# Pair loads as one 128-partition transfer, and four early pairs loaded ahead of a weight, in an attention + channel-mix kernel

## The chip, the cores and the metric

The kernel runs on one core of one Trainium2 chip. The metric is the device time of one execution in microseconds (us), lower is better. Five engines work side by side, each through its own fixed list of instructions: PE (TensorE), DVE (VectorE), ACT (ScalarE), POOL (GpSimd) and SP (SyncE, which here only issues DMAs). A DMA can be issued from SP's or from ACT's instruction list ("SPq", "ACTq" in the rows).

## The reference

Inputs are q, k, v of 8 batches x 8 heads x 576 positions x 64, s (8 x 8 x 576), two mixing vectors and three float64 weights, w_k (512 x 1024), w_v (1024 x 512) and w_r (512 x 512).

```python
# attention, per batch and head
cum    = cumsum(maximum(s, 0))
bias   = minimum(-(cum[:, None] - cum[None, :]), 0)
scores = where(causal, -1e9, q @ k.T / sqrt(64) + bias)
attn   = softmax(scores)            # rows, with 1e-9 in the divisor
x      = concat_heads(attn @ v)     # (8, 576, 512)
# channel mix
xk = mu_k * x + (1 - mu_k) * shift(x);  xr = mu_r * x + (1 - mu_r) * shift(x)
out = sigmoid(xr @ w_r) * (maximum(xk @ w_k, 0) ** 2 @ w_v)
```

## The kernel before, in words

**Pairs and visits.** Heads are treated two at a time; a pair is two heads of one batch. `visits` (L1356) lists the work on attention: first the four pairs of batch 0 in two parts each, part A (query positions 0 to 319, visits 0 to 3) and then part Z (320 to 575, visits 4 to 7), then 28 whole pairs of batches 1 to 7. The 8 visits of batch 0 are "plain": q and k go to the scores matmul as float32 (L817), with the row of prefix sums of s as a 65th partition of k. The 28 others are "split" pairs: every operand is taken apart in a high and a low part, and two matmuls (L828) make the scores.

**Loads of a pair.** `load_plain` (L668) fills a tile "KH" and a tile "G", two buffers each, with k and q of a plain visit in partitions 0 to 63 (L681). For visit 0 each head is a transfer of its own, head 0 from ACT's queue and head 1 from SP's. Partition 64 of k is the prefix-sum row. Visit 0 makes its own from s (L675, scans at L700); visit 1 copies it from the scan over all heads (L530, DMA at L709); later visits read it back from the DRAM copy `whole_d` (written at L536, read at L716). `load_turned` (L723) fills a tile "raw" (two buffers, one for q and one for k) of a split pair: the same 64 rows go to partitions 0 to 63 and again to 64 to 127, in two transfers of 288 KB (L729). `split_qk` (L737) makes from them KH and G (ACT, L769 and L782) and the low parts KL and G (POOL, L773 and L796). KL and a second copy of q, G2, lie in four fixed tiles, two KL and two G2, whose upper 64 partitions are cleared and set once by `constant_rows` (six memsets on POOL, L507 and L510).

**Weights.** `load_weight` (L568) loads a block of 512 KB of float64 words (L578) and makes float32 high and low parts of it: one ACT instruction (L603), four on DVE (L608, L615, L619, L626), one on ACT (L632) and one on POOL (L634). There are 8 blocks of w_k, 4 of w_r and 8 of w_v.

**Attention and channel mix.** For each visit and head: scores on PE, a bias, mask and row minimum on DVE (L845), exponents on ACT (L863), normalization on POOL (L899, L877) with a reciprocal on DVE (L904), transposes on PE (L921, L935), values on PE (L1068 plain, L1082 split), result to DRAM (L1437). `channel_mix` (L1152) runs over 18 chunks of 256 positions: mixing on ACT and DVE (L1173, L1184), then matmuls with w_k (L1236), w_r (L1278) and w_v (L1303). Where PE would have nothing to do early on, filler matmuls on an identity (L425) are put in its list.

**Order.** Every instruction is a task of a planner (`Plan`). `forward` (L145) makes a list schedule from estimated durations and due times, `backward` (L262) gives new due times from it, and `run` (L309) takes the best of 40 rounds and emits the instructions in that order. So each engine, and SP's list of DMAs too, has one fixed order, found for the whole kernel at once. A set of dependencies for each task keeps the order legal; at L1476 the w_v loads are made dependent on the first load of x for chunk 0.

Of the kernel before, what the change touches and what calls it, by code (L numbers as in the profile page):

```python
# [54 lines left out]
class Plan:  # L55
# [14 lines left out]
    def __init__(self):  # L70
        self.tasks, self.slots, self.due = [], {}, 0.0
        self.columns, self.idle, self.busy_from = {}, None, None
        self.ports = {}
# [71 lines left out]
    def forward(self, due):  # L145
# [6 lines left out]
        start = [0.0] * n  # L152
        for i, (_, _, _, deps, _, _) in enumerate(self.tasks):
            missing[i] = len(deps)
            for d in deps:
                users[d].append(i)
        engines = list(dict.fromkeys(t[0] for t in self.tasks))
# [22 lines left out]
        while len(order) < n:  # L180
# [71 lines left out]
            order.append(i)  # L252
            for u in users[i]:
# [8 lines left out]
    def backward(self, start):  # L262
# [4 lines left out]
        for t in self.tasks:  # L267
            for d in t[3]:
# [8 lines left out]
        for _ in range(n):  # L277
# [17 lines left out]
            for d in deps:  # L295
                k, _, _, _, _, land = self.tasks[d]
                gap = self.SELF[k] if k == e and e != "SP" else self.AFTER[k] + self.BEFORE[e]
                if k == "SP" or k == "PE":
# [26 lines left out]
def forgetting_attention_then_channel_mix(  # L325
# [15 lines left out]
    nc = tc.nc  # L341

    B, H, D, S = q.shape
    DM, DF = moe_w_k.shape
    P = 128
    NP = H // 2
# [126 lines left out]
    late, LATE = [], ("v",)  # L473
# [11 lines left out]
    KLs = [fixed(const.tile([P, 2, S], F32R, name=f"KL{i}")) for i in range(2)]  # L485
    G2s = [fixed(const.tile([P, 2, S], F32R, name=f"G2{i}")) for i in range(2)]
    turns = [0]
# [80 lines left out]
    def load_weight(name, c, o, w, due, x):  # L568
# [17 lines left out]
        if name in LATE:  # L586
            late.append(i)
        plan.due = due
# [79 lines left out]
    def load_plain(n, src, b, hp, a, e, tag):  # L668

        x = sbuf([P, 2, e - a], tag, 2)  # L670
# [7 lines left out]
        for js in ((0, 1), (1, 2)) if n == 0 else ((0, 2),):  # L678
            first = n == 0 and js[0] == 0
            (dma if not first else aside)(  # L680
                lambda js=js, queue=nc.scalar if first else nc.sync: queue.dma_start(  # L681
                    x.get()[0:64, js[0] : js[1]],
                    src[b, 2 * hp + js[0] : 2 * hp + js[1], :, a:e].rearrange("h d t -> d h t"),
                ),
                [], [(x, (j, 0)) for j in range(*js)], 580 * (js[1] - js[0]) * (e - a) / S,
            )
        if tag == "G":
            if n < 2:
# [34 lines left out]
    def load_turned(src, b, hp, a, e, tag, apart):  # L723

        x = sbuf([P, 2, e - a], "raw", 2)
        for r in range(2):
            for js in ((0, 1), (1, 2)) if apart else ((0, 2),):
                dma(
                    lambda r=r, js=js: nc.sync.dma_start(  # L729
                        x.get()[64 * r : 64 * r + 64, js[0] : js[1]],  # L730
                        src[b, 2 * hp + js[0] : 2 * hp + js[1], :, a:e].rearrange("h d t -> d h t"),
                    ),
                    [], [(x, (j, r)) for j in range(*js)], 580 * (js[1] - js[0]) * (e - a) / S,
# [783 lines left out]
```

## Time and profile before

| | us |
|---|---|
| median of 3 runs | 862.51 (860.14 to 863.93) |
| the profiled execution's own time | 861.32 |
| its span (first to last instruction) | 859.5 |
| PE busy in the span | 844.3 |
| ACT / DVE / POOL busy | 668.0 / 654.6 / 425.8 |

In the rows, a time is in us from the start of the span. "Busy" of PE counts modelled ends of pipelined matmuls, so that a busy PE isn't one at its peak. [...] The chain of waits is the work that ended last, followed back from the last instruction: at each step to what released it, or to the instruction before it on its engine. In a timeline row, the brackets give how long the engine idled before the instruction and what ended that. A DMA row in a timeline is its issue.

### The profile page before, as it was taken

How to read it: one execution, taken by the hardware profiler on the slowest of the kernel's cores; microseconds unless marked ns; L12 is line 12 of the kernel's file. 1: busy time of each engine (PE TensorE's matmuls, PEld its weight loads, DVE VectorE, ACT ScalarE, POOL GpSimd, SP SyncE). 2: the span in 40 equal slices, each digit the busy share in tenths (PEclk: the TensorE clock that was granted, in tenths of full speed). 3: DMA queues.
4: the chain of work that ended last, by engine and by line, in shares of the span. 5: the costliest groups of instructions: out<-in, count | busy, mean ns of one | idle time of the engine just before them, and what ended most of it. 6: DMA issues, size and time to landing. Idle time of an engine off the chain costs nothing.

```text
span 859.5 us, 16968 instructions
## 1 busy us (share of the span) xinstructions
PE 844.3 (98%) x5379; PEld 733.5 (85%) x5379; DVE 654.6 (76%) x2191; ACT 668.0 (78%) x1809; POOL 425.8 (50%) x654
## 2 busy tenths in 40 slices
PE   8999899999999999999999999999999999999998
PEld 5568688888899898989898989898989998987896
DVE  7997989878887887788878787788778777546431
ACT  4988999989988898889888897888787877435421
POOL 7756787686655564455665466454654632000000
PEclk9999999999999999999999999999999999999999
DMA  7998355554454444534444535252525120111100
GB/s 203 261 223 256 106 130 153 134 136 128 120 151 94 117 122 103 126 100 132 115 117 105 136 99 150 71 150 59 141 77 149 44 65 15 44 45 35 40 25 25
DMA packets 52761, 96.69 MB, mean 112 GB/s; under 512 B 7502, under 2 KB 20820, under 8 KB 52672
## 3 DMA queue, kind: packets, MB, share of 16 engines
q1 hardware_dynamic: 52512, 95.45, 42.3%
q8 instruction: 42, 0.69, 0.3%
q14 instruction: 47, 0.39, 0.2%
q10 hardware_dynamic: 160, 0.16, 0.1%
HBM read 67.85 MB, written 19.48 MB: 102 GB/s over the span
## 4 chain that ended last, share of the span: by engine, by line
PE 83%; DVE 6%; ACT 6%; DMA 2%; issue 1%; POOL 1%; SPq 0%; ACTq 0%; DVEq 0%; POOLq 0%
PE m L1303 21%; PE m L1236 20%; PE m L1278 10%; PE s L828 9%; PE po L1082 8%; PE t L921 7%; PE po L1068 3%; PE s L817 3%; DVE W L845 2%; PE t L935 1%; ACT W L863 1%; ACT xp L1173 1%; DVE pl L965 1%; DVE xp L1184 1%; DMA KH<-raw 1%
## 5 line engine op out<-in xcount | busy, mean ns | idle before, releaser
L1236 PE MATMUL m<-xh,w_k 128*128 128x256 f32 x1152 | 228.6, 285 | 2.5 <-DVE kl L1265 2.5
L863 ACT ACTIVATE W<-W,nm 64x64 f32<-64x64 f32 (+4 forms) x320 | 179.0, 561 | 25.0 <-DVE nm L845 23.9
L1303 PE MATMUL m<-w_v,kh 128*128 128x512 f32 x576 | 197.9, 401 | 0.0
L1236 PEld LDWEIGHTS m<-xh,w_k 128*128 128x128 f32 x1152 | 184.4, 188 | 4.7 <-DVE kl L1265 2.8
L877 POOL TENSOR_SCALAR W<-W,rinv 128x192 f32<-128x192 f32 (+4 forms) x320 | 166.7, 542 | 29.4 <-DVE rinv L904 26.5
L1236 PE MATMUL m<-xl,w_k 128*128 128x256 f32 x576 | 163.4, 284 | 0.1
L845 DVE CUSTOM_DVE_ANT_0 W<-s,causal 128x448 f32<-128x448 f32 (+4 forms) x320 | 127.5, 409 | 33.4 <-PE s L828 27.0
L1303 PEld LDWEIGHTS m<-w_v,kh 128*128 128x128 f32 x576 | 107.0, 188 | 17.6
L965 DVE TENSOR_TENSOR pl<-t,ph 128x512 fp32r<-128x512 f32 x224 | 103.8, 481 | 15.4 <-ACT ph L961 9.4
L1303 PE MATMUL m<-w_v,kl 128*128 128x512 f32 x288 | 114.9, 399 | 0.0
L921 PE MATMUL t<-ident,W 128*128 128x128 f32 x640 | 112.5, 275 | 0.5 <-DVE pl L965 0.2
L1236 PEld LDWEIGHTS m<-xl,w_k 128*128 128x128 f32 x576 | 108.6, 188 | 2.2 <-issue 0.6
L1184 DVE SCALAR_TENSOR_TENSOR xp<-x,mu,xp 128x256 f32<-128x256 f32 (+3 forms) x192 | 79.9, 416 | 36.1 <-ACT xp L1173 34.4
L1173 ACT ACTIVATE xp<-x,mu 128x256 f32<-128x256 f32 (+3 forms) x192 | 81.0, 422 | 29.4 <-DVE xl L1207 10.8
L828 PE MATMUL s<-KH,G 128*64 128x64 f32 (+1 forms) x336 | 97.4, 310 | 3.1 <-DVE nm L845 2.9
L1278 PE MATMUL m<-w_r,xh 128*128 128x512 f32 x288 | 99.5, 404 | 0.3
L796 POOL TENSOR_TENSOR G<-raw,G 64x1152 fp32r<-64x1152 f32 x28 | 75.0, 2677 | 46.0 <-issue 25.4
L961 ACT CAST ph<-t 128x512 fp32r<-128x512 f32 x224 | 89.4, 424 | 8.8 <-PE t L921 7.1
L828 PE MATMUL s<-KL,G 128*64 128x64 f32 x336 | 95.7, 297 | 0.0
L921 PEld LDWEIGHTS t<-ident,W 128*128 128x128 f32 x640 | 79.1, 141 | 12.9 <-issue 1.7
L899 POOL TENSOR_SCALAR rinv<-sums 128x5 f32<-128x5 f32 (+2 forms) x72 | 17.3, 241 | 133.3 <-ACT W L863 129.0
L773 POOL TENSOR_TENSOR KL<-raw,KH 64x1152 fp32r<-64x1152 f32 x28 | 74.9, 2675 | 15.2 <-ACT KH L769 14.8
(106 smaller groups left out, 1729.3 us busy)
## 6 DMA issues: line engine op xcount, KB each, us to landing
raw<-in_q SPq DMA_DIRECT2D x56, 288.0 KB
raw<-in_k SPq DMA_DIRECT2D x56, 288.0 KB
out<-g SPq DMA_DIRECT2D x36, 256.0 KB
vn<-in_v SPq DMA_DIRECT2D x28, 320.0 KB
x_d<-xT SPq DMA_DIRECT2D x28, 288.5 KB
G<-G SPq DMA_DIRECT2D x28, 288.0 KB
x<-x_d SPq DMA_DIRECT2D x12, 514.0 KB
w_k<-in_moe_w_k SPq DMA_DIRECT2D x8, 512.0 KB
```

The lines of the kernel that those rows point to most:

```text
L828: lambda x=x, g=g, K=K: nc.tensor.matmul(ps.get()[:m, :w], g.get()[:, h % 2, q0 : q0 + m], K.get()[:, h % 2, k0 : k0 + w], start=x == 0, s ...
L845: lambda a=a, e=e, at=at, i=i: nc.vector.tensor_tensor_reduce(out=W.ap[:m, at : at + e - a], in0=ps.get()[:m, a - k0 : e - k0], in1=causal ...
L863: lambda: nc.scalar.activation(W.ap[:m, :n], W.ap[:m, :n], AF.Exp, bias=nm.get()[:m, 3 * t + mi : 3 * t + mi + 1], scale=-1.0, accum_out=s ...
L877: lambda: nc.gpsimd.tensor_scalar(out=to, in0=W.ap[:m, :n], scalar1=rinv.get()[:m, t : t + 1], scalar2=1.0, op0=ALU.mult, op1=ALU.mult,),
L921: lambda: nc.tensor.transpose(ps.get()[0:m, place : place + P], pt[t].ap[:, lead(t) + k0 : lead(t) + k0 + m], ident.ap),
L961: act(lambda: nc.scalar.copy(strips(ph), src()), [ps], [(ph, k) for k in ks], n * m, ports="P>S")
L965: lambda: nc.vector.tensor_tensor(out=strips(pl), in0=src(), in1=f32(strips(ph)), op=ALU.subtract),
L1173: lambda n=n, o=o, i=i, to=to: nc.scalar.activation(to(), x.get()[:, c, o + i + 1 : o + i + 1 + n], AF.Copy, scale=mu.ap[:, which, c : c + 1],
L1184: lambda n=n, o=o, i=i, to=to: nc.vector.scalar_tensor_tensor(out=to(), in0=x.get()[:, c, o + i : o + i + n], scalar=mu1.ap[:, which, c : ...
L1236: lambda u=u, f=f, c=c, n=n, w=w, x=x: nc.tensor.matmul(ps.get()[:, u * CT : (u + 1) * CT], weight["k", c, f // 4].get()[:, w, f % 4 * P : ...
L1278: lambda c=c, n=n, x=x, w=w: nc.tensor.matmul(ps.get(), x.get()[:, c, ts], weight["r", c, 0].get()[:, w], start=c == 0 and n == 0, stop=c ...
L1303: lambda f=f, n=n, x=x, w=w: nc.tensor.matmul(ps.get(), x.get()[:, f, ts], weight["v", f, 0].get()[:, w], start=f == 0 and n == 0, stop=f ...
```

## The change

There are four edits.

1. The host stores q and k by pairs, with the 64 rows of both heads written twice, so that `load_turned` fills all 128 partitions of "raw" in one transfer of 576 KB, where there were two of 288 KB. Bytes moved are the same.
2. Visits 2 and 3 get buffers of their own for k and q, in the memory of what are later the third and fourth fixed tiles; these take their tags "KL2", "KL3", "G22" and "G23". Their loads are issued from ACT's queue. The fixed KL and G2 tiles of the split pairs become these tiles, and `constant_rows` moves from the start to behind visit 3, since its tiles are in use until then.
3. The 8 loads of w_k come, in the planner's order, behind the issue of all q and k loads of visits 0 to 3 (`behind`, `AHEAD`).
4. The w_v loads come behind the issue of chunk 0's first load of x, where the planner had them wait for its landing.

```diff
-    KLs = [fixed(const.tile([P, 2, S], F32R, name=f"KL{i}")) for i in range(2)]
-    G2s = [fixed(const.tile([P, 2, S], F32R, name=f"G2{i}")) for i in range(2)]
-    turns = [0]
+    KLs, G2s = [], []
+    turns, ahead = [0], []
...
+        if name == "k":
+            after.append(i)
...
     def load_plain(n, src, b, hp, a, e, tag):
 
-        x = sbuf([P, 2, e - a], tag, 2)
+        if n in (2, 3):
+            x = sbuf([P, 2, e - a], ("KL" if tag == "KH" else "G2") + str(n), 1)
+        else:
+            x = sbuf([P, 2, e - a], tag, 2)
...
-            first = n == 0 and js[0] == 0
-            (dma if not first else aside)(
+            first = n == 0 and js[0] == 0 or n in (2, 3)
+            i = (dma if not first else aside)(
                 lambda js=js, queue=nc.scalar if first else nc.sync: queue.dma_start(
                     x.get()[0:64, js[0] : js[1]],
-                    src[b, 2 * hp + js[0] : 2 * hp + js[1], :, a:e].rearrange("h d t -> d h t"),
+                    src[b, hp, 0:D, js[0] : js[1], a:e],
                 ),
...
+            if n < AHEAD:
+                ahead.append(i)
         if tag == "G":
-            if n < 2:
+            if n < 4:
                 pool(lambda: nc.gpsimd.memset(x.get()[64:65], 1.0), [], rows, 2 * (e - a), 36)
...
-    def load_turned(src, b, hp, a, e, tag, apart):
+    def load_turned(src, b, hp, a, e):
 
         x = sbuf([P, 2, e - a], "raw", 2)
-        for r in range(2):
-            for js in ((0, 1), (1, 2)) if apart else ((0, 2),):
-                dma(
-                    lambda r=r, js=js: nc.sync.dma_start(
-                        x.get()[64 * r : 64 * r + 64, js[0] : js[1]],
-                        src[b, 2 * hp + js[0] : 2 * hp + js[1], :, a:e].rearrange("h d t -> d h t"),
-                    ),
-                    [], [(x, (j, r)) for j in range(*js)], 580 * (js[1] - js[0]) * (e - a) / S,
-                )
+        dma(
+            lambda: nc.sync.dma_start(
+                x.get(), src[b, hp, :, :, a:e]
+            ),
+            [], [(x, (j, r)) for j in range(2) for r in range(2)], 1900 * (e - a) / S,
+        )
         return x
...
-    plan.due = 25000.0
-    constant_rows()
...
+        if n == 4:
+            for i in (2, 3):
+                KLs.append(sbuf([P, 2, S], f"KL{i}", 1, F32R))
+                G2s.append(sbuf([P, 2, S], f"G2{i}", 1, F32R))
+            constant_rows()
...
+    for i in after:
+        plan.behind[i] = set(ahead)
     for i in late:
-        plan.tasks[i][3].add(first_load[0])
+        plan.behind[i] = {first_load[0]}
...
         if name in ("q", "k"):
-            a = a.transpose(0, 1, 3, 2)
+            B, H, S, D = a.shape
+            a = a.reshape(B, H // 2, 2, S, D).transpose(0, 1, 4, 2, 3)
+            a = np.concatenate([a, a], axis=2)
```

In the planner, a task "behind" others may start once they have been issued; it doesn't wait for their data. `aside`, used for loads from ACT's queue, takes 1 ns of SP in the planner's estimate.

## Rows read from the trace of the kernel before

**Rows 1.** The page's first part: busy time of each engine, its share of the span, and the number of instructions.
```profile
PE 844.3 (98%) x5379; PEld 733.5 (85%) x5379; DVE 654.6 (76%) x2191; ACT 668.0 (78%) x1809; POOL 425.8 (50%) x654
```
**Rows 2.** The view by windows, core 0: the stretch, its length, busy time of PE, PEld, DVE, ACT and POOL with the number of instructions, granted clock, mean busy share of the 16 DMA engines, GB/s.
```profile
0.00:15.00 15.00, 11.49 (x52) 7.62 (x52) 8.69 (x26) 4.58 (x12) 11.70 (x32) 0.89 0.79 209
15.00:60.00 45.00, 44.84 (x229) 26.73 (x230) 42.99 (x144) 41.12 (x143) 32.29 (x62) 1.00 0.88 233
60.00:90.00 30.00, 30.00 (x187) 23.64 (x186) 23.68 (x61) 26.05 (x61) 14.58 (x19) 1.00 0.83 244
90.00:160.00 70.00, 66.16 (x427) 56.16 (x427) 62.86 (x230) 65.39 (x184) 57.58 (x82) 0.98 0.47 121
160.00:700.00 540.00, 537.91 (x3556) 483.63 (x3555) 437.75 (x1559) 461.49 (x1259) 302.70 (x447) 1.00 0.45 115
700.00:859.00 159.00, 153.88 (x937) 135.68 (x935) 78.62 (x175) 69.33 (x155) 6.98 (x15) 1.00 0.11 34
```
**Rows 3.** The same view for the filler matmuls of L425 alone: the stretch, its length, busy time of PE and PEld with numbers, clock, DMA share, GB/s.
```profile
15.00:60.00 45.00, 5.98 (x35) 3.23 (x35) 1.00 0.88 233
0.00:15.00 15.00, 8.02 (x40) 5.15 (x40) 0.89 0.79 209
```
**Rows 4.** The chain of waits, 0 to 16 us: start, us, what.
```profile
1.54 3.03 DMA raw<-in_s
...
7.34 7.57 DMA KH<-raw
```
**Rows 5.** Timeline of SP's queue, 0 to 17 us: start of the issue, us that it took on SP, line, transfer.
```profile
2.13 0.69 SPq L681 DMA_DIRECT2D KH<-in_k  x1
2.87 0.59 SPq L578 DMA_DIRECT2D w_k<-in_moe_w_k  x1
3.50 0.47 SPq L681 DMA_DIRECT2D G<-in_q  x1
4.01 0.59 SPq L578 DMA_DIRECT2D w_k<-in_moe_w_k  x1
4.64 0.66 SPq L681 DMA_DIRECT2D KH<-in_k  x1
5.34 0.60 SPq L681 DMA_DIRECT2D G<-in_q  x1
5.99 0.62 SPq L578 DMA_DIRECT2D w_k<-in_moe_w_k  x1
...
14.24 0.65 SPq L681 DMA_DIRECT2D KH<-in_k  x1
15.23 0.61 SPq L716 DMA_DIRECT2D KH<-whole_d  x1
```
**Rows 6.** Timeline of ACT, 0 to 10 us, its DMA issues among it.
```profile
0.72 0.55 ACTq L681 DMA_DIRECT2D KH<-in_k  x1
1.30 0.61 ACTq L681 DMA_DIRECT2D G<-in_q  x1
1.94 1.28 ACT L603 ACT_TABLE_LOAD   x1 [1.94 <-issue]
9.23 0.63 ACT L603 ACTIVATE m<-w_k 128x512 f32<-128x512 f32 x1 [6.01 <-DMA w_k<-in_moe_w_k]
9.79 0.33 ACT L863 ACTIVATE W<-W,nm 64x64 f32<-64x64 f32 x1
```
**Rows 7.** Timeline of DVE, 7 to 14 us.
```profile
7.36 0.08 DVE L845 DVE_READ_ACCUMULATOR2_ANT nm<- 64x1 f32 x1
...
9.89 0.70 DVE L608 TENSOR_SCALAR m<-m 128x512 f32<-128x512 f32 x1 [1.21 <-ACT m L603]
...
12.77 0.70 DVE L608 TENSOR_SCALAR m<-m 128x512 f32<-128x512 f32 x1 [0.52 <-ACT m L603]
13.77 0.42 DVE L845 CUSTOM_DVE_ANT_0 W<-s,causal 128x256 f32<-128x256 f32 x1 [0.30 <-PE s L817]
```
**Rows 8.** Timeline of PE, 0 to 16 us: the scores of visit 0's second head begin with the first row, those of visit 1 with the second.
```profile
9.85 0.30 PE L817 MATMUL s<-KH,G 65*64 65x64 f32 x2 [1.55 <-DMA G<-in_q]
...
15.04 0.82 PE L817 MATMUL s<-KH,G 65*64 65x64 f32 x4 [0.17 <-DMA KH<-raw]
```
**Rows 9.** Three stretches in the view by windows (columns as in rows 2): the first loads; one k of a split pair, 0.59 MB, in partitions 0 to 63 and then 64 to 127; and a stretch in which w_v blocks move, in 128 partitions.
```profile
5.00:15.00 10.00, 8.32 (x38) 5.37 (x36) 7.80 (x25) 3.30 (x11) 7.56 (x18) 0.83 0.99 257
176.50:180.00 3.50, 3.50 (x23) 3.00 (x23) 2.74 (x12) 3.22 (x12) 3.30 (x5) 1.00 0.72 169
66.00:70.00 4.00, 4.00 (x30) 3.47 (x29) 2.46 (x9) 3.72 (x9) 3.21 (x4) 1.00 1.03 403
```
**Rows 10.** The chain of waits, 160 to 176 us, around the only load of a split pair that the chain names.
```profile
166.53 2.69 POOL G L796
169.23 3.49 DMA raw<-in_q
```
**Rows 11.** All instructions of line L729, the loads of the split pairs: ns min/median/max on SP.
```profile
L729 SPq DMA_DIRECT2D raw<-in_q x56: 595/620/2086, 49.4 to 658.9; - x56
L729 SPq DMA_DIRECT2D raw<-in_k x56: 595/600/1637, 55.4 to 656.8; - x56
```
**Rows 12.** Timeline of POOL, 5 to 14 us: the six memsets of `constant_rows` and what follows.
```profile
5.63 2.05 POOL L507 MEMSET KL<- 64x1152 f32 x2
7.62 2.05 POOL L507 MEMSET G<- 64x1152 f32 x2
9.61 2.36 POOL L510 MEMSET G<- 3x1152 f32 x2
...
13.83 0.24 POOL L899 TENSOR_SCALAR rinv<-sums 128x3 f32<-128x3 f32 x1 [1.52 <-ACT W L863]
```
**Rows 13.** Another stretch in the view by windows (columns as in rows 2), from about visit 3's last scores to the first split pair's KL.
```profile
30.00:75.00 45.00, 45.00 (x247) 29.75 (x245) 39.42 (x120) 40.98 (x120) 29.43 (x46) 1.00 0.87 244
```
**Rows 14.** Timeline of PE, 90 to 160 us: the two longest of its six waits there.
```profile
98.38 0.36 PE L828 MATMUL s<-KH,G 128*128 128x192 f32 x1 [1.53 <-DVE nm L845]
...
145.00 0.39 PE L1236 MATMUL m<-xh,w_k 128*128 128x256 f32 x1 [1.07 <-DVE kl L1265]
```

More of the change, by code (lines that the diff above doesn't have):

```diff
@@ L72, in __init__ @@
         self.columns, self.idle, self.busy_from = {}, None, None
-        self.ports = {}
+        self.ports, self.behind = {}, {}
     def buffer(self, pool, shape, dtype, tag, bufs):
@@ L152, in forward @@
         start = [0.0] * n
+        followers = {}
         for i, (_, _, _, deps, _, _) in enumerate(self.tasks):
-            missing[i] = len(deps)
+            first = self.behind.get(i, set()) - deps
+            missing[i] = len(deps) + len(first)
             for d in deps:
                 users[d].append(i)
+            for d in first:
+                followers.setdefault(d, []).append(i)
         engines = list(dict.fromkeys(t[0] for t in self.tasks))
@@ L252, in forward @@
             order.append(i)
+            for u in followers.get(i, ()):
+                ready_at[u] = max(ready_at[u], s + ns)
+                missing[u] -= 1
+                if not missing[u]:
+                    heapq.heappush(coming[self.tasks[u][0]], (ready_at[u], u))
             for u in users[i]:
@@ L266, in backward @@
         left = [0] * n
-        for t in self.tasks:
-            for d in t[3]:
+        for i, t in enumerate(self.tasks):
+            for d in t[3] | self.behind.get(i, set()):
                 left[d] += 1
@@ L294, in backward @@
             free[e] = at[i] = s + ns
-            for d in deps:
+            for d in deps | self.behind.get(i, set()):
                 k, _, _, _, _, land = self.tasks[d]
                 gap = self.SELF[k] if k == e and e != "SP" else self.AFTER[k] + self.BEFORE[e]
+                if d not in deps:
+                    gap = land = 0.0
                 if k == "SP" or k == "PE":
@@ L341, in forgetting_attention_then_channel_mix @@
     nc = tc.nc
-    B, H, D, S = q.shape
+    B, NP, _, _, S = q.shape
+    H, D = v.shape[1] * 2, v.shape[-1]
     DM, DF = moe_w_k.shape
     P = 128
-    NP = H // 2
     NC = DM // P
@@ L472, in forgetting_attention_then_channel_mix @@
     first_load = []
-    late, LATE = [], ("v",)
+    late, after, LATE = [], [], ("v",)
     mu = fixed(const.tile([P, 2, NC], F32, name="mu"))
@@ L1359, in forgetting_attention_then_channel_mix @@
     PLAIN = 8
+    AHEAD = 4
     HEAD = 11200.0
@@ L1396, in load @@
         loaded[n] = (
-            load_turned(q, b, hp, q0, q1, "G", False),
-            load_turned(k, b, hp, 0, q1, "KH", False),
+            load_turned(q, b, hp, q0, q1),
+            load_turned(k, b, hp, 0, q1),
         )
```

## The prediction, made before the changed kernel had run

> **What bounds the kernel now.** I read the page's busy times first, then the view by windows in a few long stretches, then the chain of waits, and then engine by engine the places that the change touches.
>
> PE is busy for 844.3 of 859.5 us [rows 1], which alone would say that nothing but less PE work helps. The windows show that this average covers four stages [rows 2]. From 160 us to the end PE is the bound (537.91 of 540 us, then 153.88 of 159), with ACT and DVE at 81 to 85% in the first of the two. From 15 to 60 us it isn't: 5.98 us of PE's time there are fillers [rows 3], while DVE is busy for 42.99 of 45 us and ACT for 41.12. Between 90 and 160 us PE waits for 3.84 us, mostly for DVE [rows 2, 14]. The first 15 us are a start: DVE has 8.69 us of work in them, PE 8.02 us of fillers. So a microsecond of loads is worth something only before 60 us, and there no more than DVE and ACT are free to take. What is won there reaches the end, since every later stage is full and only moves forward.
>
> Two waits make the start. One is the row of prefix sums for visit 1: its DMA is issued at 7.34 and lands 7.57 us later [rows 4], though it is tiny, because k, q and three blocks of w_k of 512 KB are ahead of it in SP's queue [rows 5] and the DMA engines are 0.99 busy from 5 to 15 us [rows 9]. The other is q of visit 0's second head, issued behind a block of w_k [rows 5]: PE waits 1.55 us for it, to 9.85 [rows 8]. A third is hidden in ACT's fixed order: the first row minimum is ready at 7.44 [rows 7], but its exponents start at 9.79, because the first instruction on w_k stands ahead of them and waits 6.01 us for its block [rows 6].
>
> **The change, part by part.** The sum is made against the profiled execution's own 861.32 us; its span is 859.5, so 1.8 us lie outside. The median of the runs shown is 1.2 us higher.
>
> *Visit 0's second head* (gain). Its q has no block of w_k ahead any more. What that can give is DVE's idle time between the first head's scores and visit 1: 1.21 + 0.52 + 0.30 = 2.0 us [rows 7]. The other end is 0, if ACT still holds the exponents behind w_k. I take the middle, -1.0.
>
> *Visit 1's row* (loss). Four transfers of 160 KB, k and q of visits 2 and 3, now move before it: 0.655 MB at 257 GB/s [rows 9] is 2.55 us later. It costs nothing where ACT and DVE have w_k to work on meanwhile; one block is four DVE instructions of 0.7 us or so [rows 7], so a single block in time covers it. That cover is the likely one, but DVE's list is fixed ahead, so some is lost: 0 to 2.55, I take +0.7.
>
> [...] In the rows, the loads that start on ACT's queue at 0.72 and 1.30 and those on SP's share one busy time of the DMA engines [rows 6, 9]; no row shows two long rows of transfers on both queues at once. [...]
>
> *Visits 2 and 3* (gain). Their k and q were issued from 14.24 on [rows 5]; now they wait for no buffer. But between 15 and 60 us DVE idles for 45 - 42.99 = 2.0 us in all [rows 2], and no wait of it is for these loads. Also, their prefix-sum rows still come by way of `whole_d`, whose read is issued at 15.23 [rows 5], and the 0.655 MB are ahead of that copy too. So 0 to 2.0; -0.5.
>
> *ACT's four issues* cost 0.55 to 0.61 us each [rows 6], 2.4 in sum, on ACT. They stand between 1.9 us and the table load, which then ends at about 5.6; the first exponents are ready at 7.44. Nothing is lost while that idle time covers them; without it, 2.4.
>
> *w_k behind the loads* (loss). In front of the first block there are now 80 KB of q, 320 KB of visit 1 and 640 KB of visits 2 and 3 more: 1.065 MB at 257 GB/s, 4.1 us. PE needs w_k only behind 60 us, so the data are not late. The loss comes only through ACT's order; it is the slow rival below, and 0 in the sum.
>
> *Split pairs' loads* (gain). The one k at 176.5 us takes 0.72 x 3.5 = 2.5 us of full DMA for 0.59 MB, 234 GB/s; blocks of w_v, in 128 partitions, move at 403 GB/s [rows 9]. At that rate a load takes 1.46 us, 1.06 less, and one issue of 0.6 us less on SP [rows 11]. There are 56 such loads, but the chain names one, 3.49 us at 169.23 [rows 10], behind a POOL instruction that frees the buffer. The others land before ACT asks for them. So 0 to 1.7; I take -1.0. SP gets 56 x 0.6 = 34 us of issues less, which is worth nothing as SP is not in the chain; what stands behind a load in SP's list (results, x, G2) starts 0.6 us earlier.
>
> *The six memsets* (loss). They take 6.46 us on POOL [rows 12]; today they lie where POOL has nothing else and even idles 1.52 us behind them. Now they fall between visit 3's scores and the first split pair's KL. In that stretch POOL is busy for 29.43 of 45 us [rows 13], so there is room for all six, and the price is that of one normalization which comes behind a memset of 2.36 / 2 = 1.2 us. If every one stood ahead of a normalization for which PE waits, it were 6.46. I take +0.2.
>
> *w_v behind x's issue.* Its loads may start some 2 to 3 us earlier in a stretch in which the DMA engines are full anyway; the conversions wait for tiles that chunk 0 still uses. Nothing.
>
> Sum: -1.0 + 0.7 - 0.5 - 1.0 + 0.2 = -1.6, so 861.3 - 1.6 = 859.7 us.
>
> One cost has no row: the planner makes the order of the whole kernel anew. What an order can win or lose is bounded by PE's waits between 90 and 160 us, 3.84 us [rows 2]: these may vanish, or come once more. I take 0, with 3.8 to both sides.
>
> **The rivals.** *Slower: ACT holds visit 0 behind a later w_k.* If the first w_k instruction keeps its place ahead of the first exponents, these start 4.1 us later than 9.79, and with them the normalizations, transposes and everything behind them on an ACT that is 91% full until 60 us [rows 2]. With one memset in the way that is 861.3 + 4.1 + 1.2 = 866.6. For it: just this wait stands in the trace. Against it: a block that is due later is more likely to be placed later. It decides from the point at which the first exponents start after 9.8 us.
>
> *Faster: the start runs without holes.* All gains at their ends, the row's delay covered: 861.3 - 2.0 - 2.0 - 1.7 = 855.6, and down to 851.8 if the 3.84 us go too. For it: DVE bounds this stage and has 4.0 us of holes, and PE 5.98 us of fillers to give up. Against it: none of those holes after 15 us is put down to a load.
>
> *The one transfer is no faster than the two.* The rows for 128 partitions are those of other blocks; if the pair loads stay at 234 GB/s, only the issue is saved, the 1.0 us is gone, and it ends at 860.7.
>
> **How the numbers follow.** Forecast 859.7: 0.36. Same speed of the transfer, 860.7: 0.10. Without holes, 855.6: 0.33. ACT held, 866.6: 0.21. The first two lie within 0.5% of 861.3 (857.0 to 865.6), which is about what a measurement of this kernel can tell from no change; the third is faster, the fourth slower. So faster 0.33, same 0.46, slower 0.21. The forecast's own range is 857 to 864. To leave out no more than 2 in 10, the range reaches down to the fast rival with the 3.8 us of the order (852) and up to the slow one (867).
>
> **What would show it.** Right: PE's wait for visit 0's second q is gone and its scores end before 11 us; visit 1's scores start between 15 and 17.6 us; first exponents near 7.5 us; the first matmul on w_k (L1236) 1 to 2 us earlier; a pair's load takes about 1.5 us of full DMA; no wait of POOL or PE on a memset. Wrong: first exponents after 9.8 us; the stretch from 15 to 60 us with less DVE work than 43 us in it; or a gain that arises behind 160 us, where I see at most 5 us of holes before the tail and none that a load would fill.

## The result, and the profile after

The changed kernel is slower: 874.6 us in the median of 6 runs (864.6 to 877.4) against 862.1 of the kernel before, a ratio of 1.0122 with a 95% interval of 1.0093 to 1.0152. (Ratios here and below leave out executions that count as disturbed, so they needn't be those of the medians; the times and counts told are of all executions.) The forecast was 859.7 and the range ended at 867.

The median hides that one and the same program takes two sorts of time, and they go with PE's granted clock, a share of the full one, averaged over an execution: two runs at 1.00 took 864.6 and 866.2 us, four at 0.982 to 0.986 took 874.4 to 877.4. So there are two things to explain, some 3 to 4 us at full clock and 10 to 13 us in the other executions. The profiled execution is one of the shorter ones (866.23 us, span 864.4); rows of it can show the first, and those of experiments have to show the second.

The windows of the changed kernel, core 0 (columns as in [rows 2], which they answer to):

```profile
0.00:15.00 15.00, 11.99 (x46) 7.21 (x46) 7.00 (x19) 3.54 (x9) 6.04 (x26) 1.00 0.86 243
15.00:60.00 45.00, 44.08 (x221) 25.70 (x222) 42.08 (x145) 40.20 (x138) 36.60 (x67) 1.00 0.74 230
60.00:90.00 30.00, 29.18 (x174) 22.26 (x173) 25.44 (x64) 25.72 (x60) 16.05 (x18) 1.00 0.74 232
90.00:160.00 70.00, 67.07 (x430) 55.30 (x429) 60.64 (x222) 64.91 (x179) 53.14 (x80) 1.00 0.40 112
160.00:700.00 540.00, 537.09 (x3544) 481.91 (x3543) 437.78 (x1556) 461.90 (x1257) 306.03 (x447) 1.00 0.40 115
700.00:864.00 164.00, 159.19 (x968) 140.31 (x966) 83.43 (x192) 73.79 (x170) 8.67 (x20) 1.00 0.11 35
```

PE still has 159.19 us of work left at 700 us, where it had 153.88. Of these 5.3 us, PE's waits between 160 and 700 us can make 0.8 (537.09 for 537.91). So nearly all is lost before 160 us. DVE does 7.00 + 42.08 us of work by 60 us, before 8.69 + 42.99, that is 2.6 us less in the stage that it bounds.

The chain of waits of the changed kernel, 0 to 17 us, answers to [rows 4] (start, us, what):

```profile
1.96 4.05 DMA KL<-in_k
...
6.02 6.51 DMA w_k<-in_moe_w_k
...
12.56 0.64 ACT m L615
...
13.21 0.70 DVE m L620
...
15.10 0.59 PE s L831 x2
```

The row of prefix sums has left the chain; the first block of w_k has taken its place. It is issued at 6.02, behind k and q of all four visits (the first piece of the chain is k of visit 2), and lands 6.51 us later. What waits for it is seen in the timelines of the changed kernel, here of ACT, DVE, POOL and PE in turn, which answer to [rows 6 to 8] (start, us, what; in brackets the idle time before and what ended it):

```profile
4.95 0.54 ACTq L696 DMA_DIRECT2D G<-in_q  x1
5.52 1.28 ACT L615 ACT_TABLE_LOAD   x1 [5.52 <-DMA raw<-in_s]
12.56 0.63 ACT L615 ACTIVATE m<-w_k 128x512 f32<-128x512 f32 x1 [5.75 <-DMA w_k<-in_moe_w_k]
13.11 0.33 ACT L877 ACTIVATE W<-W,nm 64x64 f32<-64x64 f32 x1
...
10.05 0.08 DVE L859 DVE_READ_ACCUMULATOR2_ANT nm<- 64x1 f32 x1
13.21 0.70 DVE L620 TENSOR_SCALAR m<-m 128x512 f32<-128x512 f32 x1 [3.09 <-ACT m L615]
13.82 0.41 DVE L859 CUSTOM_DVE_ANT_0 W<-s,causal 128x256 f32<-128x256 f32 x1
...
15.92 0.25 POOL L913 TENSOR_SCALAR rinv<-sums 128x3 f32<-128x3 f32 x1 [9.05 <-ACT W L877]
...
11.23 1.27 PE L831 MATMUL s<-KH,G 65*128 65x320 f32 x2
12.30 1.92 PE L436 MATMUL xp<-ident 128*128 128x256 bf16 x9
15.10 0.59 PE L831 MATMUL s<-KH,G 65*128 65x192 f32 x2 [0.88 <-DVE nm L859]
```

The first exponents start at 13.11, before at 9.79. DVE stands idle for 3.09 us, with scores of visit 0 next in its list behind the instruction on w_k; it comes to them only at 13.82. PE fills with 9 filler matmuls and then waits 0.88 us. PE's waits for visit 0's second q (1.55 us) and for visit 1's row are gone.

The 1.00 in the clock's column of the first window has to be read with care. In these traces the records of the clock begin with its first change, here a rise at 13.9 us, and a view counts what lies before the first record as 1.00. The nine fillers of the row above took 1.92 us, 0.21 us each; in an execution shown below 33 of them took 3.77 us, 0.11 us each. So PE was at the lower of the two levels in its records, 0.50, up to some 14 us, and a mean clock of 1.00 doesn't exclude a start at the lower level.

The six memsets now stand between 27 and 46 us on POOL. In the same timeline, the first two and the last of them, and then PE's only two waits in that stretch:

```profile
27.69 1.05 POOL L517 MEMSET G<- 64x1152 f32 x1 [0.33 <-POOL w_k L646]
29.13 1.05 POOL L517 MEMSET KL<- 64x1152 f32 x1
...
44.58 1.05 POOL L520 MEMSET G<- 3x1152 f32 x1
...
31.99 0.33 PE L949 MATMUL t<-ident,W 128*128 128x128 f32 x1 [0.27 <-POOL sums L821]
43.01 0.33 PE L935 MATMUL t<-ident,W 128*128 128x128 f32 x1 [0.46 <-POOL W L891]
```

### The profile page after: what moved, and what is told of

The parts are those of the page before. It is cut to its first block, busy times and chain, and to the rows that moved or that the text cites. A ratio compares the mean times of both kernels' runs of the same rounds, so it can differ in the third digit from the quotient of the medians.

```text
span 864.4 us, 16879 instructions
## 1 busy us (share of the span) xinstructions
PE 848.6 (98%) x5375; PEld 732.7 (85%) x5375; DVE 656.4 (76%) x2191; ACT 670.1 (78%) x1809; POOL 426.5 (49%) x656
## 4 chain that ended last, share of the span: by engine, by line
PE 72%; DVE 12%; ACT 8%; POOL 3%; issue 3%; DMA 1%; ACTq 0%; POOLq 0%; DVEq 0%
PE m L1250 19%; PE m L1317 18%; PE m L1292 9%; PE s L842 8%; PE po L1096 6%; PE t L935 6%; DVE W L859 3%; PE po L1082 2%; DVE pl L979 2%; ACT W L877 2%; PE s L831 2%; DVE xp L1198 2%; ACT xp L1187 2%; PE t L949 1%; POOL G L810 1%
## 5 line engine op out<-in xcount | busy, mean ns | idle before, releaser
L877 ACT ACTIVATE W<-W,nm 128x448 f32<-128x448 f32 (+4 forms) x320 | 178.7, 560 | 24.7 <-DVE nm L859 21.3
L1096 PE MATMUL po<-ph,V 128*128 128x448 f32 x280 | 77.9, 309 | 0.9 <-DVE ph L1044 0.8
```

The costliest lines, as they stand in the source:

```text
L877: lambda: nc.scalar.activation(W.ap[:m, :n], W.ap[:m, :n], AF.Exp, bias=nm.get()[:m, 3 * t + mi : 3 * t + mi + 1], scale=-1.0, accum_out=s ...
L1096: lambda: nc.tensor.matmul(po.get()[: P if both else 64, at + q0 - base : at + q0 - base + m], V.get()[:, kb, 2 * j : 2 * j + (2 if both e ...
```

## The experiments

All ratios are to the kernel before, run on the same chip. "Full clock" means a mean granted clock of 0.995 or more over the execution, by the records, which can hide a low start. Three runs above 900 us, and one of the kernel before (1735 us), are left out of the groups told below: one of 1647 us, of the kernel without edit 3, read a clock of 1.00; the other two are named at their kernels.

### Again, and the parts of the change

*The changed kernel, unchanged*, to see whether the two sorts of time come back and what a profile of a longer execution shows.

> The changed kernel once more, unaltered. Its six runs fell in two groups, 864.6 and 866.2 us at a mean granted clock of 1.0, and 874.4 to 877.4 us at 0.982 to 0.986; the profile so far is of the first group. [...] Rival 'noise': the groups don't come back, and the runs spread evenly between 864 and 878. I expect the two groups again, with more runs in the second, median 874.

868.7 us in the median of 11 runs, 1.0074 (1.0044 to 1.0103). Together with the first six: 7 of 17 runs at 864.3 to 866.2, 3 at 868.7 to 869.1 and 7 at 874.2 to 878.6 (clock 0.979 to 0.986). The profiled execution is one of the middle group. Its PE, in a timeline:

```profile
10.71 1.18 PE L436 MATMUL xp<-ident 128*128 128x256 bf16 x9
13.87 0.60 PE L831 MATMUL s<-KH,G 65*128 65x192 f32 x2 [1.98 <-DVE nm L859]
...
16.36 0.42 PE L935 MATMUL t<-ident,W 128*128 128x128 f32 x1
...
24.79 0.27 PE L935 MATMUL t<-ident,W 128*128 128x128 f32 x1
```

ACT's first w_k instruction starts 1.2 us earlier here, at 11.32, and still PE waited 1.98 us instead of 0.88. Here the nine fillers take 1.18 us: the clock had risen early, at 5.2 us by its records. Behind the wait a transpose takes 0.42 us, and 0.27 us at 24.79: the clock fell again at 15.4 us, and up to 22.2 us PE ran at half clock while it was needed (0.54 in the window from 15 to 20 us). In the profiled execution above, which rose late, no such fall came.

*Edit 1 alone*, the one transfer for each k and q of a split pair; all else as before.

```diff
 # the kernel before, with only load_turned and the host's layout changed
+            x.get(), src[b, hp, :, :, a:e]
```

> The kernel before with edit 1 alone (one load of 128 partitions per q or k of a split pair). Theory 'start': the loss arises in the first 60 us from edits 2 and 3, so this one costs nothing: 860 to 863, ratio 0.996 to 1.001. Rival 'order': any new order of this planner costs 3 to 5 us and can set off the clock; then 865 to 875 here too. In either case a pair's load takes about 1.5 us of full DMA where two took 2.5.

859.9 us, 0.9983 (0.9967 to 0.9999), a gain of 1.5 us with an interval of 0.1 to 2.8, and all 11 runs at full clock. The transfer itself is faster, by less than I took. This is the changed kernel's window around one q, of 0.59 MB:

```profile
177.00:181.00 4.00, 4.00 (x26) 3.53 (x25) 2.77 (x12) 3.54 (x12) 3.62 (x8) 1.00 0.48 152
```

0.48 x 4 = 1.9 us of full DMA, where the two transfers took 2.5 [rows 9] and the forecast had 1.46.

*Without edit 3*, so w_k isn't held behind the loads.

```diff
-    for i in after:
-        plan.behind[i] = set(ahead)
```

> The changed kernel without edit 3: w_k blocks need not stand behind the pair loads. On ACT the first w_k instruction still stands ahead of the first exponents, but its block is the second load on SP's queue after the first k, so that it lands near 9 us as in the kernel before. Theory 'ACT held by a late w_k': the first exponents start near 9.8 us again and 2.5 us of the loss go; 861 to 864 in its fast group. Rival 'memsets': the loss comes from POOL between 27 and 46 us, then 865 to 867 here.

863.8 us, 1.0025 (1.0002 to 1.0048); 862.4 to 863.9 at full clock, and up to 879.1 at 0.979. The expected 861 to 864 at full clock came, some 2 us less than with edit 3, in another order; with edits 1, 2 and 4 some loss and some of the low clock remain.

*The first two w_k instructions of ACT behind visit 0's exponents.*

```diff
+    for i in first_words[:2]:
+        plan.behind[i] = set(exps[:6])
```

> The changed kernel with one order more: the first ACT instructions on the first two w_k blocks come behind visit 0's six exponents. Theory 'ACT held by a late w_k': exponents start near 9 us instead of 13.1, DVE's idle 3.1 us at 10 us is gone, the loss of the start goes: 860 to 863 in the fast group. Theory 'clock': if the wait of PE at 14 to 15 us sets off the slow group, that group goes as well. Rival 'memsets': the memsets are where they were, 865 to 867.

867.7 us, 1.0076 (1.0047 to 1.0105), all runs at 0.994 or less. The exponents do start early, at 8.77, and it doesn't help. In the timelines of this kernel, ACT and PE:

```profile
8.77 0.45 ACT L879 ACTIVATE W<-W,nm 128x192 f32<-128x192 f32 x1 [2.47 <-DVE nm L861]
...
13.61 0.98 PE L833 MATMUL s<-KH,G 65*128 65x192 f32 x2 [1.89 <-DMA KH<-raw]
```

PE runs out of scores sooner and waits 1.89 us for visit 1's row. The wait has moved, and the clock falls: it is at 0.50 from 15 to 20 us in this execution. So putting the exponents first doesn't bring the time back, which speaks against the slow rival; what ACT's order costs by itself, at full clock, this kernel can't show.

*Edit 1, and all w_k instructions of ACT behind the first head's exponents*, the same question without edits 2 to 4.

```diff
+    for i in first_words[:8]:
+        plan.behind[i] = set(exps[:3])
```

> Edit 1 alone (859.9 us) with the first ACT instructions on w_k behind the exponents of visit 0's first head. There ACT waits 4.2 us for the first block with exponents behind it. Theory 'ACT held by w_k' says the hold costs time wherever it stands: 857.5 to 859. Rival: what counts is how much work DVE gets before 15 us, from w_k as well as from scores; the hold costs nothing here, 859 to 862.

863.4 us, 1.0022 (1.001 to 1.0034), some 3.5 us more than edit 1 alone and above both expectations; the three runs that read 1.00 took 863.2 to 863.4. Exponents ahead of w_k are no gain in this kernel either: in the profiled execution DVE does 3.36 us of work between 10 and 15 us instead of 4.93, and the clock is at 0.54 there.

*Edit 1, and w_k behind the loads of visits 0 and 1.*

```diff
-    AHEAD = 4
+    AHEAD = 2
```

> The first edit alone, with one thing more: the w_k loads come behind the q and k loads of visits 0 and 1 (which have buffers in any case), and nothing else of edits 2 to 4. Theory (later w_k takes DVE's and ACT's work out of 8 to 15 us, and PE's waits then let its clock fall): 861 to 864, DVE busy less than 4.5 of 5 us from 10 to 15, and some runs at a lower clock. Rival (w_k's place costs nothing, as the prediction had it): 859.5 to 860.5, in all runs at a clock of 0.995 or more.

859.7 us, 0.9973 (0.9945 to 1.0002), all six runs between 859.0 and 860.2, no worse than edit 1 alone. The theory that I held by then, that any later w_k costs time, falls. Its first block reaches ACT at 9.53, as against 12.56 in the changed kernel, which has the 640 KB of visits 2 and 3 ahead of it as well. The clock falls here too, behind a wait of PE of 1.39 us, but is back by 15 us (0.66 from 10 to 15 us, 1.00 from 15 to 20).

### The clock

*Some fillers:* 6 ahead of the third and 12 ahead of the sixth scores product, to see whether the longer executions get rarer when PE's wait ahead of the sixth is filled.

```diff
+            if i in self.plain:
+                seen += 1
+                for _ in range({3: 6, 6: 12}.get(seen, 0)):
+                    self.idle()
```

> The changed kernel with 6 more fillers on PE ahead of the third and 12 ahead of the sixth scores product, where it waits for DVE in some executions up to 2 us. [...] Rival 'chance' (clock falls whatever PE does): the same split as before. If the fillers are in the way, all come 1 to 2 us later.

865.6 us, 1.0067 (1.004 to 1.0093): 5 of 9 runs at 865.2 to 865.6, the others at 868.5 to 878.7. PE still waited 1.60 us, up to 14.64. The profiled execution is a long one, 875.2 us. Its windows show what such an execution looks like:

```profile
10.00:15.00 5.00, 3.40 (x27) 2.65 (x26) 2.25 (x9) 2.77 (x9) 0.00 (x0) 1.00 1.02 391
15.00:20.00 5.00, 4.95 (x21) 2.94 (x20) 3.72 (x17) 3.73 (x14) 3.11 (x10) 0.58 0.65 217
20.00:25.00 5.00, 5.00 (x14) 2.70 (x13) 3.31 (x12) 2.55 (x11) 1.61 (x3) 0.50 0.96 272
25.00:30.00 5.00, 5.00 (x17) 2.72 (x16) 2.73 (x11) 3.05 (x11) 2.42 (x7) 0.50 0.03 12
30.00:35.00 5.00, 5.00 (x16) 2.10 (x15) 2.43 (x9) 1.71 (x7) 2.02 (x3) 0.50 0.01 2
35.00:40.00 5.00, 5.00 (x19) 3.27 (x19) 2.89 (x14) 3.91 (x14) 3.51 (x6) 0.53 0.73 211
40.00:45.00 5.00, 5.00 (x28) 2.90 (x26) 3.96 (x16) 3.42 (x16) 4.26 (x9) 1.00 0.40 132
```

PE is busy for 3.40 of 5 us, then the clock falls and stays down until nearly 40 us. In that time PE is busy all through, with 14 to 19 matmuls in 5 us where it does 28 at full clock, and DVE and ACT idle behind it. What PE can lose by that is 5 x (0.42 + 0.5 + 0.5 + 0.5 + 0.47) = 12 us; the execution took 9.8 us more than the five shortest of this kernel.

*More fillers*, 8 and 24, in the changed kernel's own order.

```diff
+                for _ in range({3: 8, 6: 24}.get(seen, 0)):
+                    self.idle()
```

> The changed kernel, its memsets in place, with 8 fillers ahead of the third and 24 ahead of the sixth scores product. Theory (two separate costs): the low clock is gone and the memsets' cost stays, 864 to 866 in nearly all executions. Rival (it was all the clock): 860 to 861.

865.9 us, 1.0052 (1.0038 to 1.0066), all five runs between 864.6 and 866.1, all at 0.999 or more. Two rows of PE's timeline, and two of the windows:

```profile
10.66 3.77 PE L441 MATMUL xp<-ident 128*128 128x256 bf16 x33
14.26 0.58 PE L836 MATMUL s<-KH,G 65*128 65x192 f32 x2
```
```profile
10.00:15.00 5.00, 5.00 (x42) 4.18 (x41) 2.64 (x9) 2.94 (x10) 0.00 (x0) 1.00 1.01 397
15.00:20.00 5.00, 4.95 (x28) 2.93 (x27) 5.00 (x24) 4.60 (x19) 4.34 (x11) 1.00 0.75 250
```

The wait ahead of 14 us is filled, and no run fell to the longer times, nor did one of the ten of a kernel below that has the same order and fillers and only its memsets elsewhere; without the fillers it was 10 of 17. The fillers compute nothing, so the 10 to 13 us were the clock's, and to keep PE at work between 8 and 16 us was enough to hold it up in these 15 runs (mean clock 0.998 or more). Which of the two filled places matters isn't parted. The 3 to 4 us at full clock stay.

*The kernel before, without any filler*, its order untouched.

```diff
-            for emit in emits.get(n, ()):
-                emit()
```

> The kernel before with its order unchanged and no filler matmuls, so PE has less work in the first 15 us and between 15 and 60 us; nothing of the change in it. Theory (what costs 9 to 13 us in about half of the executions of the changed kernel is a granted clock of half speed that lasts into the stretch in which PE is needed): the clock is at half speed for longer, beyond 15 us, and the time goes up to 866 to 878 us, with a lower mean clock in the runs that take longer. Rival (the clock falls along with waits that cost the time by themselves, and does nothing of its own): 861 to 862, as the fillers compute nothing.

Two runs took 863.6 and 864.4, four 876.8 to 880.6. So the kernel before can be had 16 to 20 us slower with not one instruction of its work changed. The lower mean clock that was expected of the long runs wasn't read: they have 0.995 to 1.00. The records can't show a clock that has yet to rise for the first time; in the profiled execution, of 864.4 us, that is at 29.0 us. The matmuls show it, in PE's timeline:

```profile
17.71 0.42 PE L919 MATMUL t<-ident,W 128*128 128x128 f32 x1
...
31.30 0.27 PE L919 MATMUL t<-ident,W 128*128 128x128 f32 x1
```

No trace shows one of the four long runs; that their clock rose later still is an inference.

### The memsets and the order

*The memsets behind chunk 0's first load of x*, for which the planner makes a new order.

```diff
+        plan.behind[i] = {first_load[0]}     # i: each of the six memsets
```

> The changed kernel with its six memsets placed behind the issue of chunk 0's first load of x (about 52 us), where POOL has room. In the changed kernel they lie between 27.7 and 45.6 us and make POOL busy for 19.5 of 21 us there; 1.4 us of PE's progress are lost between 30 and 45 us. Theory 'memsets': those 1.4 us come back, executions with the full clock at 862.5 to 863.5 instead of 864.3 to 866. Rival 'w_k late alone': the place of the memsets doesn't matter, 864 to 865. The groups of executions with a lower clock should remain, since they are set off before 20 us.

864.3 us, 1.0025 (1.0 to 1.005). Three runs took 859.8 to 860.2, the nine others 861.4 to 878.0. I read that as 4 us for the memsets. The next runs show that it was mostly something else.

*The same without edit 3.*

> The same place for the memsets, and w_k not held behind the pair loads (edit 3 undone): edits 1, 2 and 4 without the two suspected costs. It was 863.8 with the memsets early. Theory 'memsets' and 'w_k late' together explain the loss: 860 to 862, as the loads alone (859.9). Rival 'something else in edit 2' (pair loads that compete with the first ones for the DMA engines, or a worse order): 863 to 864.

873.5 us, 1.0128 (1.0091 to 1.0166), no run above 0.99, and neither expectation met. In this order PE waits 3.33 us for ACT up to 20.90, and the profiled execution (877.0 us) has the clock at 0.50 from 20 to 50 us.

*Edit 1, and the memsets behind visit 3's last scores.*

```diff
+            plan.behind[ pool(lambda x=x: nc.gpsimd.memset(...)) ] = {plain[-1]}
```

> The first edit alone, with one thing more: the six memsets of the fixed tiles come behind the last scores product of visit 3, where they stand in the changed kernel, and nothing else of edits 2 to 4. The first edit alone took 859.9 us. Theory (the memsets fill a POOL that is full between 26 and 47 us, and PE waits for its normalizations): 863 to 865 us, with POOL busy for over 19 of the 21 us from 26 to 47. Rival (they cost no more than one normalization, +0.2 us, as the prediction had it, and the 4 us that the late memsets gave came from another order of the whole): 859.5 to 861.

At full clock 860.0 to 860.7 us (three runs), 878.0 and 881.8 at 0.973 and 0.970, and one of 1016.2 at 0.751. The memsets by themselves cost at most 1 us here; the 863 to 865 that I expected didn't come. The profiled execution, of 878.0 us, has the clock at 0.50 from 10 to 55 us.

*Late memsets and 8 and 24 fillers*, with a new order.

> The changed kernel with the memsets behind chunk 0's first load of x (859.8 to 860.2 us in the executions at full clock, 864.3 us in the median) and with 8 fillers ahead of the third and 24 ahead of the sixth scores product, to close PE's two waits between 8 and 15 us. Theory (those waits are what lets the clock fall): 860 to 861 in the median and few runs above 863. Rival (the clock falls whatever PE does there): runs at 864 and 870 as often as without fillers, or later scores by the fillers' own time, 862 to 866.

860.2 us, 0.9979 (0.9947 to 1.001); five runs between 859.4 and 861.1, and one of 913.9 at a mean clock of 0.851, of which there is no trace: the fillers don't guard against everything. In the five, all four edits are compatible with the 859.7 of the forecast.

To part the memsets from the order, three kernels kept the changed kernel's very order on all engines but for what is named.

*Only the six memsets moved, as one block; and the same with 8 and 24 fillers.*

```diff
+            if i == self.mark:              # chunk 0's first load of x
+                for x in self.last:         # the six memsets
+                    self.tasks[x][2]()
```

> The changed kernel with the very order that its planner found, except that the six memsets are taken out of their places and put right ahead of chunk 0's first load of x. Theory (the memsets cost about 4 us where they stand, because POOL is full there): executions at full clock at 860 to 861, where the changed kernel's are at 864.3 to 866.2; executions with a clock below 0.99 as often as before, at 870 or more. Rival (another order of the whole, which the earlier kernel with late memsets also had, gave those 4 us): 864 to 866 at full clock.

> The same as the kernel with only the memsets moved, with 8 fillers ahead of the third and 24 ahead of the sixth scores product besides. Theory (two separate costs, the memsets and the clock): 860 to 861 in nearly all executions. Rival (order): 864 to 866.

871.8 us, 1.0113 (1.0094 to 1.0132), and 870.2, 1.0103 (1.0088 to 1.0117): both sides were wrong. In the second kernel, the timelines of POOL, DVE and PE between 51 and 60 us:

```profile
51.71 2.05 POOL L528 MEMSET KL<- 64x1152 f32 x2
53.71 2.06 POOL L528 MEMSET G<- 64x1152 f32 x2
55.71 2.05 POOL L532 MEMSET G<- 3x1152 f32 x2
57.81 0.10 POOL L1487 MEMSET xT<- 64x2 f32 x1
58.00 0.22 POOL L927 TENSOR_SCALAR rinv<-sums 128x2 f32<-128x2 f32 x1
...
58.26 0.17 DVE L932 RECIPROCAL rinv<-rinv 128x2 f32<-128x2 f32 x1 [3.63 <-POOL rinv L927]
...
58.84 1.02 PE L844 MATMUL s<-KH,G 65*128 65x448 f32 x2 [2.91 <-DVE nm L873]
```

A normalization stands behind 6 us of memsets, DVE's reciprocal waits 3.63 us for it and holds the row minimum behind it, PE waits 2.91 us, and from 60 to 65 us its clock is at 0.54. This is the dear end of what the forecast had for the memsets, 6.46 us if each stood ahead of a normalization for which PE waits, and the lower clock comes on top.

*The memsets moved singly*, three POOL instructions from one to the next, with 8 and 24 fillers.

```diff
+                if since % 3 == 2:
+                    self.tasks[late.pop(0)][2]()
```

> The changed kernel in its own order with the 8 and 24 fillers (865.9 us in the median with its memsets in place), with the six memsets moved behind chunk 0's first load of x, but one at a time with three POOL instructions from one to the next, not as one block. If the memsets cost 1.5 us where they stand (what PE had done more by 45 us in the kernels without them there): 864 to 865. If they cost all that separates 865.9 from the 860.2 of the kernel with late memsets, fillers and another order: 860 to 861. If nothing: 865.5 to 866.5.

864.4 us, 1.0033 (1.0021 to 1.0045), all ten runs at 0.998 or more. Against the same kernel with the memsets in place that is 865.92 - 864.36 = 1.6 us, though the two intervals overlap. PE's waits of 0.27 and 0.46 us for POOL, shown with the result, are about half of it. But the moved memsets aren't free either. The timelines of POOL and PE in this kernel:

```profile
56.15 1.05 POOL L536 MEMSET KL<- 64x1152 f32 x1
57.30 0.74 POOL L913 TENSOR_SCALAR W<-W,rinv 128x576 f32<-128x576 f32 x1
...
58.10 0.55 PE L957 MATMUL t<-ident,W 128*128 128x128 f32 x3 [1.26 <-POOL W L913]
```

One memset stands right ahead of a normalization, and PE waits 1.26 us for that. So 1.6 us is what the move gained, not all that the memsets cost; about 1 us more is theirs here.

*The order and nothing else*, for the kernel before and for the changed one: the planner's least time for an issue on SP is another.

```diff
-        return plan.add("SP", max(520, ns), emit, reads, writes, land=1300)
+        return plan.add("SP", max(500, ns), emit, reads, writes, land=1300)
```

> The kernel before with another order and nothing else: the planner's least time for an issue on SP is 500 ns where it was 520, so that its 40 rounds go other ways. It measures what an order is worth by itself. Theory (the order makes part of the changed kernel's loss): a time that differs from 861.1 by 1 to 4 us to either side. Rival (orders of this planner are all alike): 860.5 to 861.7.

> The changed kernel with the same 500 ns for 520, so that it has all four edits in another order. Theory (part of its loss is the order found, and its start lets the clock fall in some executions): executions at full clock at 860 to 864, and some above 868. Rival (all of the loss belongs to the edits): 864.3 to 866.2 at full clock as before.

The kernel before: six runs at 859.6 to 860.8 and four at 870.1, 876.5, 877.9 and 884.1, with clocks of 0.969 to 0.988. In its first order, 5 of 98 runs were at 0.99 or less, and those took 866.7 to 869.7. The changed kernel: 863.1 and 863.4 at full clock, five runs at 865.9 to 866.3 (0.991 to 0.993), three at 875.0 to 875.9 (0.980 to 0.982). None of the edits is needed for the long executions; another order is enough. The profile of the kernel before in this order is of a short execution, without a wait of PE between 2 and 22 us; that of the changed kernel, of 865.96 us, has the clock at 0.50 from 10 to 20 us.

## Why the prediction was wrong, point by point

**The step that failed** is the bound on what no row showed: "the planner makes the order of the whole kernel anew. What an order can win or lose is bounded by PE's waits between 90 and 160 us, 3.84 us". At full clock that bound held: with all four edits and the memsets late, one order gave 860.2 us and another 864.4, 4.2 apart. But an order also sets PE's waits in the first 16 us, and the prediction priced a wait there at no more than its own length. In the repeated changed kernel a wait of 1.98 us was followed by 7 us at half clock, in the one with 6 and 12 fillers a wait of 1.60 us by 24 us, and that execution took 9.8 us more. So the changed kernel ended beyond the range, at 874.6. The kernel before in another order took 870 to 884 us in 4 of 10 runs, with no edit in it; in single executions the cost of an order was thus -2 to +23 us. What was left out is a clock that stood in the rows, 0.89 in [rows 2] and 0.83 in [rows 9], and has no term in the sum. That its low stretches did no harm in the kernel before, where they lay before 15 us, didn't mean that they would in another order.

The changed kernel began at the lower clock and rose at 13.9 us in one execution and at 5.2 us in another. A late rise by itself cost nothing that shows here (859.7 us for the kernel before in another order, with the first rise at 14.7 us; PE did 22 matmuls there from 10 to 15 us and 29 from 15 to 20); what cost 10 to 13 us of 865, 1.2 to 1.5%, is a fall behind the first rise.

*Visit 0's second head* (-1.0). Its q arrives in time and PE's wait for it is gone, but DVE's holes grew: 3.09 us behind w_k in place of 2.0, and the head's last scores begin at 15.10, where they were to end before 11. No gain.

*w_k behind the loads* (0, and the slow rival). The rival's condition came true, with first exponents 3.3 us later (4.1 were worked out), and its 866.6 us lie near the 864.3 to 866.2 at full clock. That is luck in part, as its mechanism doesn't carry the loss: exponents put first gave 867.7 and 863.4 us. What these kernels share is that DVE and PE had little work in 10 to 15 us, whichever of w_k and the row is late; that this is the cause is argued. Two of the three signs of being wrong that the prediction names were there, 13.11 for the first exponents and 42.08 us of DVE's work from 15 to 60 us; but the first stood, at 10.08, in the kernel with w_k behind two visits' loads too. That w_k comes behind two visits' loads costs nothing (859.7).

*Visit 1's row* (+0.7). Of the kernels with edit 2, PE waited for it only in the one with exponents first, where it was there by 13.61; before it landed at 7.34 + 7.57 = 14.91 [rows 4]. So the 0.655 MB ahead of it made it no later: in the first 15 us the DMA engines moved 243 GB/s, before 209. More bytes moved in the same time, so what those loads would have cost the row at an unchanged rate no run shows.

*Visits 2 and 3* (-0.5). Not shown to give anything. The kernels without them, edit 1 alone and w_k behind two visits' loads, lost nothing.

*Split pairs' loads* (-1.0). Right in sign and about in size, -1.5 (-2.8 to -0.1), though a load became faster by 0.6 us of full DMA and not by 1.06, and the one load in the chain [rows 10] has gone from it. But another order of the kernel before gave 859.6 to 860.8 at full clock as well, so this gain can't be told from an order's.

*The memsets* (+0.2). Mis-sized: about 1.6 us in the order found, by two intervals that overlap, and more if the wait at 58 us counts. The room that I read was a mean over 30 to 75 us [rows 13]; they fell between 27 and 46, where POOL was full (busy for 19.49 us from 26 to 47). In this kernel POOL is busy for 36.60 of the 45 us, before 32.29.

What remains at full clock, with the fillers and the memsets moved singly, is 864.4 - 861.4 = 3 us, about 1 of them PE's wait behind a memset, against -1.8 (-4.6 to +0.9) in the other order that had late memsets and the same fillers. I put the rest down to the order, since two orders of the same work differ by that much, but that is argued; at which places of 15 to 160 us it is lost I couldn't show. Nor is it settled what decides, in one execution and not in the next, that the clock falls.

## What to carry to other kernels

Where PE has little to do, as in a start, ask of every wait that moves there what the clock does after it, and price a stretch at the lower clock at half of its length as far as PE is needed in it (a filler took 0.21 us there and 0.11 at full clock). Look at the time and mean clock of every run, not at one profiled execution, and check the clock by the duration of one form of matmul: medians of a kernel near that edge say which way its executions fell. And where a planner makes the whole order anew, run the old kernel in another order first; what that moves is the least that an edit's own effect has to exceed.

## What the runs showed of the hardware

Every trace of a kernel with fillers begins at the lower clock: the first 19 fillers, from 1.83 us on, take 3.5 to 4.2 us (25 in one kernel, 4.9), about 0.2 us each. By the records the first rise came at 4.5 to 7.1 us in 15 of the 20 traces, at 11.2 to 14.7 in four, and at 29.0 us in the kernel before without fillers. Of the 15 that rose early, 12 lacked the 8 and 24 fillers, and 11 of these fell again between 8.8 and 18.8 us. Each of these falls lies within a wait of PE of 0.6 to 3.3 us or less than 2 us behind one. The twelfth, edit 1 alone, had a wait of 0.91 us and didn't fall, so a wait isn't all that it takes. The three with the fillers didn't fall before 60 us, nor did the five that rose late before 58 us. That a late rise spares an execution the fall would fit the two traces of the changed kernel; it is a regularity of these traces, not a cause shown.

A fall lasted from 3.4 us (the kernel before, and the one with w_k behind two visits' loads) to 48 us (edit 1 and the memsets moved). Once down, the clock stayed down although PE was never idle by its rows: 5.00 of 5 us busy from 20 to 35 us at 0.50 in the kernel with 6 and 12 fillers, and from 10 to 55 us in the one with edit 1 and the memsets moved. Why it stayed down isn't shown.

The mean of the granted clock isn't always to be trusted. It leaves out a low start, as in the kernel before without fillers, where a transpose takes 0.42 us, as long as at 0.50 elsewhere, in a stretch that reads 1.00. With late memsets two runs of 864.5 and 870.6 us read 1.00, as did those of 859.8 to 860.2; whether a late rise is behind them no trace shows. And in the trace of the repeated changed kernel the records read 0.95 where a transpose takes 0.27 us, as at 1.00 elsewhere. The duration of one form of matmul is the better witness.
